# Turned r and k without their 32 lanes of zeros, in two transfers of 48 lanes; W's halves, steps and products spread another way

## The chip, the cores and the metric

The kernel runs on one core of a Trainium2 chip. The metric is the device time of one execution in microseconds (us). Before the change three runs took 636.44, 637.63 and 646.48 us: a median of 637.63.

## The reference, cut to what matters

Three parts follow one another: an attention with a decaying state over 768 steps, a mixture of experts that skips tokens, and a dense two-branch MLP.

```python
# r, k, v: (4, 8, 768, 48); w, u: (8, 48)
for t in range(S):
    kt, vt, rt = (k[:, :, t], v[:, :, t], r[:, :, t])
    cur = np.einsum('bhd,bhe->bhde', u[None] * kt, vt)
    y[:, :, t] = np.einsum('bhd,bhde->bhe', rt, state + cur)
    state = w[None, :, :, None] * state + np.einsum('bhd,bhe->bhde', kt, vt)
...
# x: (3072, 384), y of all heads; 8 experts, d_ff 1024
skip_score = x @ w_skip          # only tokens above 0 go to an expert
e_idx = np.argmax(xc @ w_gate, axis=1)
h = np.maximum(xc[mask] @ w1[e], 0.0)
y[mask] = gate_w[mask, None] * (h @ w2[e])
...
# 384 -> 1024, two branches; w3: 1024 x 1024, w_out: 1024 x 384
h = (x @ w1) * (x @ w2) @ w3
return h @ w_out
```

## The kernel before, in words

The attention works in chunks of 64 tokens. A step handles one chunk of two batches of all 8 heads; there are NT = 24 steps, and the loop `for n in range(NT - 2)` has 22 rounds, 0 to 21 here (the 13th is round 12); what is left follows as a list of hand-ordered steps. All is in a manual schedule: each engine runs its instructions in the order in which the Python code emits them, and semaphores join the engines.

Round n does this. `prep(n + 2)` (VectorE) multiplies TB, the turned r and k of a step (128 lanes, of which 0 to 47 and 64 to 111 hold the 48 dims of two batches), by the decay tables UT into FK. `scores(n + 1)` (TensorE) makes the 64 x 64 scores of each head from FK's 48 lanes, `evac` (VectorE) masks them into Fs. `prep_k`, `prep_m` (GpSimd), `bonus` (VectorE, z) and `prep_v` (ScalarE, zv) make the u term. `y_mm(n)` (TensorE) multiplies Fs by v and FK by the copied state Ss; `x_out(n)` adds zv into xg, which goes to the DRAM tensor xm in two transfers; `x_trans` and `logits` turn xg and make the router's logits; `ds_mm(n)` adds into the state S. Every transfer here is issued by SP, in the order of the code: `load_t(n + 4)` brings TB (three buffers, each waiting for z), `load_v(n + 4)` KV.

Beside it the last two weights of the MLP are multiplied ahead of time, W = w3 @ w_out. Its inputs come in 12 jobs of two halves each (`load_part`, LW[n] halves in round n); each job takes three steps of ScalarE and VectorE (`w_step`, at three places of a round, WN[n]); its 64 products, fp32 of 128 x 384, are made by `keep(k)`, which in round n stands behind y_mm and behind x_trans, with WK[n] products wanted at each. If the order has no product ready, `keep` puts in fillers instead, two bf16 matmuls on zeros (`dummy`, zb) for each half of a product. 26 such fillers warm TensorE up ahead of round 0.

Behind the 22 rounds come the last routing steps, with products and fillers between them, a gather of the first expert's tokens (xr), `trans_x(0)`, which turns them into xh and xl, and then what is left of the products. The experts' first matmul (hp) follows.

Of the kernel before, what the change touches and what calls it, by code (L numbers as in the profile page):

```python
# [19 lines left out]
P = 128  # L20
NB, NH, NS, HD = 4, 8, 768, 48
D = NH * HD
NTOK = NB * NS
CH = 64
NC = NS // CH
NT = NTOK // P
# [15 lines left out]
TP = (1,) * 11  # L42
GROUPS = [6, 6, 4, 4, 4]
W3B = 5
WK = [(1, 0)] * 13 + [(3, 2)] * 9
WN = [(0, 0, 0)] * 3 + [(0, 0, 1)] + [(1, 0, 1), (1, 0, 0)] * 4 + [(1, 0, 1)] + [(1, 1, 1), (1, 0, 1), (1, 0, 1)] * 3
LW = [1] * 11 + [2] * 11
KW = 16
NRING = 8
RG = 3  # L50
# [11 lines left out]
def fused_kernel(ctx, tc, att, kv, wt, u, wg, we, w3, wo, w12, r, k, v, wu, out):  # L62
    nc = tc.nc
# [146 lines left out]
    def load_expert(e, q):  # L210
        raw = stg[(4 * e + q) % 3 // 2].tile([P, 2, 2 * D], F32, name="raw")
        nc.sync.dma_start(out=raw, in_=we[e, :, 2 * q:2 * q + 2, :])
        return raw
# [29 lines left out]
    with tc.manual_schedule():  # L243
# [7 lines left out]
        TB = [ac.tile([P, 2, NH, CH], F32, name=f"TB{j}") for j in range(3)]  # L251
        un = ac.tile([P, NH, HD], F32, name="un")

        def load_t(n):
            return nc.sync.dma_start(out=TB[n % 3].rearrange("p a h t -> p (a h t)"), in_=att[n])

        def load_v(n):
            c, bp = divmod(n, 2)
# [4 lines left out]
        wf = [0]  # L263
        mask = ac.tile([P, CH], F32, name="mask")
        zb = con.tile([P, DQ], BF16, name="zb")
        nc.vector.memset(zb, 0.0)

        spare = [None]
# [5 lines left out]
        for _ in range(NWARM):  # L274
            dummy(DQ)
        load_t(0)
        load_t(1)
        nc.sync.dma_start(out=un.rearrange("p h d -> p (h d)"), in_=u)
        load_v(0)
# [33 lines left out]
        def load_part(gate=None):  # L313
            x = next(w_parts, None)
            if x and gate:
                behind(x, gate, "transfers one after the other")
# [9 lines left out]
        for i in range(6):  # L326
            wn = pw[:, i - 1] if i else wc
            n = 1 << i
# [5 lines left out]
        nc.vector.reciprocal(out=cc, in_=pw[:, 5])  # L334
        cb = cc[:, :, None].to_broadcast([P, NH, CH])
        nc.vector.tensor_tensor(out=UT[:, 0, 0], in0=Ur, in1=cb, op=ALU.mult)
        half = [slice(64 * q, 64 * q + 64) for q in range(2)]
        dims = [slice(64 * q, 64 * q + HD) for q in range(2)]
        KU = ac.tile([P, 2, NH, HD], F32, name="KU")

        def table_k(c2):
# [46 lines left out]
        def prep(n):  # L388

            t = TB[n % 3]  # L390
            FK = FK_[n] = wk.tile([P, 2, NH, CH], F32, name="FK", bufs=3)
            return nc.vector.tensor_tensor(out=FK, in0=t, in1=UT[:, n // 2 % 2], op=ALU.mult)

        def behind(later, earlier, reason="two operands from SBUF each"):

            tc.add_manual_dep(later.ins, earlier.ins.name, mybir.DependencyInfo(
                mybir.DependencyClass.Sync, mybir.DependencyReason.DATA), reason=reason)

        def scores(n):
            FK = FK_[n]  # L400
            sc = ps_1.tile([P, 512], F32, tag="sc", name="sc").rearrange("p (h t) -> p h t", h=NH)
            for h in range(NH):
                for m, d in zip(half, dims):
                    nc.tensor.matmul(sc[m, h], FK[d, 1, h], FK[d, 0, h], start=True, stop=True)  # L404
            return sc

        def evac(n, sc):
            Fs = Fs_[n] = wk.tile([P, NH, CH], F32, name="Fs")
            nc.vector.tensor_tensor(out=Fs, in0=sc, in1=mask[:, None, :].to_broadcast([P, NH, CH]), op=ALU.mult)

        def prep_k(n):

            c, bp = divmod(n, 2)
            if c < NC - 1:
                kd = kd_[n] = wk.tile([P, NH, HD], F32, name="kd")
                return nc.gpsimd.tensor_tensor(out=kd, in0=KV[bp][c % 2][:, 1], in1=KU[:, c % 2], op=ALU.mult)

        def prep_m(n, eng=nc.gpsimd):

            c, bp = divmod(n, 2)  # L420
            m = P_[n] = wk.tile([P, NH, HD], F32, name="m")
            first = eng.tensor_tensor(out=m, in0=KV[bp][c % 2][:, 0], in1=un, op=ALU.mult)
            eng.tensor_tensor(out=m, in0=KV[bp][c % 2][:, 1], in1=m, op=ALU.mult)
            return first

        def bonus(n):
            z = z_[n] = wk.tile([P, 32], F32, name="z")[:, 0:NH]
            return nc.vector.tensor_reduce(out=z, in_=P_.pop(n), axis=AX.X, op=ALU.add)  # L428
# [11 lines left out]
        def state_copy(n):  # L440
            c, bp = divmod(n, 2)
            s = S[bp]
            if c == 0:
                return
            if c % 2 == 0:
                nc.vector.tensor_tensor(out=s, in0=s, in1=w128[:, :, None].to_broadcast([P, NH, HD]),
                                        op=ALU.mult)
            nc.scalar.copy(out=Ss[bp], in_=s)
# [263 lines left out]
        def w_step(k):  # L712
            for _ in range(k):
                next(wprep, None)
# [10 lines left out]
        def w_ready():  # L725
            done.update(fresh[0])
            fresh[:] = fresh[1:] + [[]]
# [71 lines left out]
        for n in range(NT - 2):  # L799
            w_ready()  # L800
            if n == NT - 3:
                raws = {q: load_expert(0, q) for q in range(2)}
            fk = prep(n + 2)
            for _ in range(LW[n] if n else 0):
                load_part(fk)
            state_copy(n + 1)
            sc = scores(n + 1)
            behind(prep_k(n + 1) or prep_m(n + 2), fk)
            if n < NT - 3:
                prep_m(n + 2)  # L810
            evac(n + 1, sc)
            z = bonus(n + 1)
            if n + 4 < NT:
                behind(load_t(n + 4), z, "transfers one after the other")
            if n == NT - 3:
                bonus(NT - 1)
            if n > 1:
                next(more_consts, None)
            w_step(WN[n][0])
            w_ready()  # L820
            y_mm(n)
            keep(4 * WK[n][0])
            run_todo()
            if n > 0:
                x_trans(n - 1)
            prep_v(n + 1)
            keep(4 * WK[n][1])
            w_step(WN[n][1])
            w_evac(0)
            x_out(n)  # L830
            ds_mm(n)
            place_mm(n % 2)
            if n + 4 < NT:
                load_v(n + 4)
            if n < NT - 3:
                place(3)
            w_step(WN[n][2])
            run_todo(n < NT - 3)
            if n > 0:
                todo.append((logits, (n - 1,)))  # L840

        a, b, g = NT - 2, NT - 1, len(groups) - 1
# [597 lines left out]
def _layout(i):  # L1440
    c = np.ascontiguousarray
    r, k, v, w, u = (i[n] for n in "rkvwu")

    def t_lay(a):
        a = a.reshape(2, 2, NH, NC, CH, HD).transpose(3, 0, 1, 5, 2, 4).reshape(NT, 2, HD, NH * CH)
        return np.pad(a, [(0, 0), (0, 0), (0, CH - HD), (0, 0)]).reshape(NT, P, NH * CH)

    def n_lay(a):
        return a.reshape(2, 2, NH, NC, CH, HD).transpose(3, 0, 1, 4, 2, 5).reshape(NT, P, D)

    wt = np.ones((P, NH), np.float32)
    for q in range(2):
        wt[64 * q:64 * q + HD] = w.T
    wg = np.concatenate([i["moe_w_gate"], i["moe_w_skip"][:, None]], 1)
    w1 = i["moe_w1"].reshape(NE, ND, P, NF, P).transpose(0, 2, 3, 1, 4).reshape(NE, P, NF, D)
    w2 = i["moe_w2"].reshape(NE, NF, P, D).transpose(0, 2, 1, 3)

    def m_lay(a):
        return a.reshape(ND, P, NF, P).transpose(1, 2, 0, 3).reshape(P, NF, D)

    def words(a):
        a = c(a)
        return a.view(np.int64) if a.dtype == np.float64 else a

    m1, m2 = m_lay(i["moe2_w1"]), m_lay(i["moe2_w2"])
    return {
        "att": c(np.concatenate([t_lay(r), t_lay(k)], -1)),
        "kv": c(np.concatenate([n_lay(r), n_lay(k), n_lay(v)], -1)),
        "r": c(r.reshape(NB * NH, NS * HD)),
        "k": c(k.reshape(NB * NH, NS * HD)),  # L1470
        "v": c(v.reshape(NB * NH, NS, 4, 12).transpose(2, 0, 1, 3).reshape(4, NB * NH, NS * 12)),
        "wu": c(np.broadcast_to(np.stack([w, u], 1), (4 * NB, NH, 2, HD)).reshape(P, 2, HD)),
        "wt": wt,
        "u": c(np.broadcast_to(u.reshape(1, D), (P, D))),
        "wg": c(wg.reshape(ND, P, 9).transpose(1, 0, 2)),
        "we": c(np.concatenate([w1, w2], -1)),
        "w3": words(i["moe2_w3"].reshape(NF, P, NF, P).transpose(0, 3, 2, 1).reshape(NF, P, FF)),
        "wo": words(i["moe2_w_out"].reshape(NF, P, D).transpose(1, 0, 2).reshape(P, NF * D)),
        "w12": words(np.concatenate([m2[..., :P], m1, m2[..., P:]], -1).reshape(P, NF * 2 * D)),
    }  # L1480
# [18 lines left out]
```

## Time and profile before

| | |
|---|---|
| runs | 636.44, 637.63, 646.48 us |
| the profiled execution | 642.96 us, span 641.2 us |
| TensorE matmuls / weight loads | busy 620.0 / 550.7 us |
| VectorE, ScalarE, GpSimd | busy 456.4, 302.9, 139.0 us |
| attention and W's products | 0 to about 189 us of the span |
| experts | about 189 to 340 us |
| MLP | about 340 to 641 us |

How to read it: start and duration in us from the span's start; `x32` merges equal instructions in a row; each fp32 matmul of the code is two records. "issue" names time in which an engine waited for nothing that the profile shows. [...]

### The profile page before, as it was taken

What the parts mean: (1) busy time and instruction counts of PE and PEld (TensorE: products, weight loads), DVE (VectorE), ACT (ScalarE), POOL (GpSimd) and SP (SyncE); (2) the same over time, 40 slices, a digit from 0 to 9 for tenths busy, and PEclk for the clock granted to TensorE, in tenths of its full rate; (3) what the DMA queues carried; (4) which work ended last, traced back from release to release, by engine and by line L of the source; (5) the groups of instructions that cost most, each with busy time, mean ns of one, the idle gap of its engine ahead of it and who ended that gap; (6) DMA issues with size and microseconds to landing.
All of it is one profiled execution on the core that took longest, in us unless ns stands there. A gap on an engine that the chain in (4) does not pass through costs nothing.

```text
span 641.2 us, 15282 instructions
## 1 busy us (share of the span) xinstructions
PE 620.0 (97%) x6309; PEld 550.7 (86%) x6309; DVE 456.4 (71%) x808; ACT 302.9 (47%) x716; POOL 139.0 (22%) x138
## 2 busy tenths in 40 slices
PE   8899999999999999999998999999999999999996
PEld 7888886777769999999997988988988988988984
DVE  9777985777568799999966963863864763763770
ACT  3666563455336666657634543442442442443430
POOL 4975462443040323214124300000000000000000
PEclk9999997999999999999999999999999999999999
DMA  7998895772537786878422002002002002001001
GB/s 297 337 348 273 275 395 178 253 268 78 173 123 248 274 276 244 291 262 263 146 69 69 2 17 82 1 18 83 1 17 83 1 17 82 2 11 39 1 2 54
DMA packets 28525, 90.60 MB, mean 141 GB/s; under 512 B 4201, under 2 KB 10490, under 8 KB 28448
## 3 DMA queue, kind: packets, MB, share of 16 engines
q1 hardware_dynamic: 26400, 84.11, 38.2%
q0 software_dynamic: 2048, 5.44, 2.6%
q8 instruction: 51, 0.84, 0.5%
q14 instruction: 26, 0.21, 0.1%
HBM read 77.81 MB, written 12.58 MB: 141 GB/s over the span
## 4 chain that ended last, share of the span: by engine, by line
PE 82%; DVE 11%; issue 4%; ACT 1%; DMA 1%; POOL 0%; ACTq 0%; DVEq 0%
PE po L1263 15%; PE xy L1225 11%; PE za L1225 10%; PE zb L1225 8%; PE wp L741 6%; PE hp L954 5%; PE y L973 5%; PE sc L404 3%; DVE elo L89 3%; PE S L474 3%; PE y L458 2%; PE y L461 2%; PE G L461 2%; PE G L458 2%; DVE hl L958 2%
## 5 line engine op out<-in xcount | busy, mean ns | idle before, releaser
L1207 DVE TENSOR_TENSOR C<-st,za 128x512 f32<-128x512 f32 x47 | 32.3, 687 | 69.7 <-ACT st L1242 69.6
L89 DVE TENSOR_TENSOR elo<-raw,ehi 128x768 fp32r<-128x768 f32 x64 | 60.6, 951 | 3.7 <-ACT ehi L88 3.4
L954 PE MATMUL hp<-xh,ehi 128*128 128x256 f32 x192 | 55.3, 290 | 1.9 <-DVE hl L958 1.6
L1263 PE MATMUL po<-pl,W_hi 128*128 128x512 f32 x144 | 56.8, 394 | 0.0
L1263 PE MATMUL po<-ph,W_hi 128*128 128x512 f32 x144 | 56.6, 393 | 0.0
L1242 ACT COPY st<-xy 128x256 f32<-128x256 f32 x47 | 17.6, 374 | 81.9 <-PE xy L1225 81.9
L1263 PE MATMUL po<-ph,W_lo 128*128 128x512 f32 x144 | 56.1, 390 | 0.0
L88 ACT CAST ehi<-raw 128x768 fp32r<-128x768 f32 x64 | 52.6, 828 | 1.6 <-DMA raw<-in_we 1.6
L954 PE MATMUL hp<-xh,elo 128*128 128x256 f32 x192 | 53.3, 279 | 0.0
L1225 PE MATMUL xy<-bxh,w12h 128*128 128x256 f32 x188 | 53.3, 283 | 0.0
L954 PE MATMUL hp<-xl,ehi 128*128 128x256 f32 x192 | 53.3, 279 | 0.0
L1225 PE MATMUL xy<-bxl,w12h 128*128 128x256 f32 x188 | 53.1, 282 | 0.0
L1225 PE MATMUL xy<-bxh,w12l 128*128 128x256 f32 x188 | 53.1, 282 | 0.0
L741 PE MATMUL wp<-wo_s,w 128*128 128x384 f32 x128 | 51.5, 531 | 0.0
L438 ACT ACTIVATE zv<-KV,z 128x48 f32<-128x48 f32 x184 | 44.0, 325 | 3.0 <-DVE z L428 3.0
L1225 PE MATMUL za<-bxh,w12l 128*128 128x512 f32 x141 | 45.1, 320 | 0.0
L1225 PE MATMUL za<-bxh,w12h 128*128 128x512 f32 x141 | 45.0, 319 | 0.0
L1225 PE MATMUL za<-bxl,w12h 128*128 128x512 f32 x141 | 44.7, 317 | 0.0
L957 ACT ACTIVATE hh<-hp 128x256 fp32r<-128x256 f32 x64 | 24.5, 383 | 40.0 <-PE hp L954 37.8
L973 PE MATMUL y<-ehi,hh 128*128 128x384 f32 x128 | 43.4, 339 | 0.0
L973 PE MATMUL y<-ehi,hl 128*128 128x384 f32 x128 | 43.2, 337 | 0.0
L973 PE MATMUL y<-elo,hh 128*128 128x384 f32 x128 | 43.0, 336 | 0.0
(249 smaller groups left out, 1688.8 us busy)
## 6 DMA issues: line engine op xcount, KB each, us to landing
raw<-in_we SPq DMA_DIRECT2D x32, 768.0 KB, 5.2
KV<-in_kv SPq DMA_DIRECT2D x24, 576.0 KB, 5.8
TB<-in_att SPq DMA_DIRECT2D x24, 512.0 KB, 6.3
raww<-in_w SPq DMA_DIRECT2D x16, 512.0 KB, 6.6
raw<-in_w SPq DMA_DIRECT2D x8, 768.0 KB, 5.9
xm<-xg SPq DMA_DIRECT2D x48, 96.0 KB, 3.3
out<-ob SPq DMA_DIRECT2D x18, 256.0 KB, 2.0
x<-xm SPq DMA_DIRECT2D x20, 192.0 KB, 3.3
```

What stands on the lines that cost most here:

```text
L88: nc.scalar.copy(out=hi, in_=raw)
L89: (eng or nc.vector).tensor_tensor(out=lo, in0=raw, in1=hi.bitcast(F32), op=ALU.subtract)
L438: nc.scalar.activation(out=zv[:, h], in_=v[:, h], func=AF.Copy, scale=z[:, h:h + 1])
L458: nc.tensor.matmul(yv[m, h], Fs[m, h], v[m, h], start=(h == 0), stop=True, skip_group_check=True)
L461: nc.tensor.matmul(yv[m, h], FK[d, 0, h], Ss[bp][d, h], start=False, stop=True, skip_group_check=True)
L741: nc.tensor.matmul(ps, w3[:, g], wo_s[:, g], start=(g == 0), stop=(g == NF - 1))
L954: nc.tensor.matmul(hp, a, b, start=(i == 0), stop=(i == 8))
L957: nc.scalar.activation(out=hh, in_=hp, func=AF.Relu)
L973: nc.tensor.matmul(ys[e, t], a[:, P * t:P * t + P], b[:, D:2 * D], start=(f == 0 and i == 0), stop=(f == NF - 1 and i == 2))
L1207: nc.vector.tensor_tensor(out=halves(C[:, 0]), in0=st[:, 0:2], in1=halves(za), op=ALU.add)
L1225: nc.tensor.matmul(o, a, m, start=first and i == 0, stop=(i == 2), skip_group_check=True)
L1263: nc.tensor.matmul(po, a[:, f, c], b, start=(i == 0), stop=(i == 3 * NF - 1))
```

## The change

r and k are no longer padded to 64 lanes in DRAM. `load_t` issues two transfers, to lanes 0 to 47 and 64 to 111, and both wait for z. The lanes between, which FK's multiplication still reads, are cleared once at the start: lanes 32 to 63 and 96 to 127 of each TB, the first buffer by VectorE ahead of zb, the other two by GpSimd. The three lists have other numbers: WK wants (2, 2) products in rounds 12 to 14; WN and LW spread steps and halves another way.

```diff
--- before.py
+++ after.py
@@ -42,9 +42,9 @@
 TP = (1,) * 11
 GROUPS = [6, 6, 4, 4, 4]
 W3B = 5
-WK = [(1, 0)] * 13 + [(3, 2)] * 9
-WN = [(0, 0, 0)] * 3 + [(0, 0, 1)] + [(1, 0, 1), (1, 0, 0)] * 4 + [(1, 0, 1)] + [(1, 1, 1), (1, 0, 1), (1, 0, 1)] * 3
-LW = [1] * 11 + [2] * 11
+WK = [(1, 0)] * 12 + [(2, 2)] * 3 + [(3, 2)] * 7
+WN = [(0, 0, 0)] * 3 + [(0, 0, 1)] + [(1, 0, 1), (1, 0, 0)] * 2 + [(1, 0, 1)] * 7 + [(1, 1, 1)] * 4 + [(1, 0, 1)] * 3
+LW = [0] + [1] * 6 + [1, 2] * 8
 KW = 16
 NRING = 8
 RG = 3
@@ -251,8 +251,17 @@
         TB = [ac.tile([P, 2, NH, CH], F32, name=f"TB{j}") for j in range(3)]
         un = ac.tile([P, NH, HD], F32, name="un")
 
+        half = [slice(64 * q, 64 * q + 64) for q in range(2)]
+        dims = [slice(64 * q, 64 * q + HD) for q in range(2)]
+
+        def clear_t(j, eng):
+
+            for q in range(2):
+                eng.memset(TB[j][64 * q + 32:64 * q + 64], 0.0)
+
         def load_t(n):
-            return nc.sync.dma_start(out=TB[n % 3].rearrange("p a h t -> p (a h t)"), in_=att[n])
+            t = TB[n % 3].rearrange("p a h t -> p (a h t)")
+            return [nc.sync.dma_start(out=t[d], in_=att[n, q]) for q, d in enumerate(dims)]
 
         def load_v(n):
             c, bp = divmod(n, 2)
@@ -263,6 +272,9 @@
         wf = [0]
         mask = ac.tile([P, CH], F32, name="mask")
         zb = con.tile([P, DQ], BF16, name="zb")
+        clear_t(0, nc.vector)
+        for j in (1, 2):
+            clear_t(j, nc.gpsimd)
         nc.vector.memset(zb, 0.0)
 
         spare = [None]
@@ -334,8 +346,6 @@
         nc.vector.reciprocal(out=cc, in_=pw[:, 5])
         cb = cc[:, :, None].to_broadcast([P, NH, CH])
         nc.vector.tensor_tensor(out=UT[:, 0, 0], in0=Ur, in1=cb, op=ALU.mult)
-        half = [slice(64 * q, 64 * q + 64) for q in range(2)]
-        dims = [slice(64 * q, 64 * q + HD) for q in range(2)]
         KU = ac.tile([P, 2, NH, HD], F32, name="KU")
 
         def table_k(c2):
@@ -801,7 +811,7 @@
             if n == NT - 3:
                 raws = {q: load_expert(0, q) for q in range(2)}
             fk = prep(n + 2)
-            for _ in range(LW[n] if n else 0):
+            for _ in range(LW[n]):
                 load_part(fk)
             state_copy(n + 1)
             sc = scores(n + 1)
@@ -811,7 +821,8 @@
             evac(n + 1, sc)
             z = bonus(n + 1)
             if n + 4 < NT:
-                behind(load_t(n + 4), z, "transfers one after the other")
+                for x in load_t(n + 4):
+                    behind(x, z, "transfers one after the other")
             if n == NT - 3:
                 bonus(NT - 1)
             if n > 1:
@@ -1442,8 +1453,7 @@
     r, k, v, w, u = (i[n] for n in "rkvwu")
 
     def t_lay(a):
-        a = a.reshape(2, 2, NH, NC, CH, HD).transpose(3, 0, 1, 5, 2, 4).reshape(NT, 2, HD, NH * CH)
-        return np.pad(a, [(0, 0), (0, 0), (0, CH - HD), (0, 0)]).reshape(NT, P, NH * CH)
+        return a.reshape(2, 2, NH, NC, CH, HD).transpose(3, 0, 1, 5, 2, 4).reshape(NT, 2, HD, NH * CH)
 
     def n_lay(a):
         return a.reshape(2, 2, NH, NC, CH, HD).transpose(3, 0, 1, 4, 2, 5).reshape(NT, P, D)
```

The start on SP's queue, where un and KV stand behind TB. `DMAHW` counters belong to SP's transfers (the number is the counter, taken in turn), `DVE` and `Pool` to VectorE and GpSimd. Before:

```order
L247 DMA wtt<-in_wt 128x8
L255 DMA TB_117<-in_att 128x1024
L255 DMA TB_118<-in_att 128x1024
L278 DMA un<-in_u 128x384
L259 DMA KV_0_111<-in_kv 128x1152
L259 DMA KV_0_113<-in_kv 128x1152
L255 DMA TB_119<-in_att 128x1024
L259 DMA KV_1_112<-in_kv 128x1152
```

Of the change:

```order
L247 DMA wtt<-in_wt 128x8
L264 DMA TB_117<-in_att 48x1024 [waits DVE_49] x2
L264 DMA TB_118<-in_att 48x1024 [waits Pool_49] x2
L290 DMA un<-in_u 128x384
L268 DMA KV_0_111<-in_kv 128x1152
L268 DMA KV_0_113<-in_kv 128x1152
L264 DMA TB_119<-in_att 48x1024 [waits DMAHW0_49,Pool_49]
L264 DMA TB_119<-in_att 48x1024 [waits DMAHW1_49,Pool_49]
L268 DMA KV_1_112<-in_kv 128x1152 [waits DMAHW2_49]
```

Each TB is two transfers, and they wait for the memsets of VectorE or GpSimd, and from the eighth transfer on for the one eight before.

TensorE in round 12, from the second half of y_mm to ds_mm (wp holds the products or the fillers, T the turned xg, S the state). Before:

```order
L461 MATMUL y<-Ss_115,FK 64x48 x16
L741 MATMUL wp_121<-wo_s,w_802 128x384
L503 MATMUL y<-wgs,xT 128x9 x3
L490 MATMUL T<-ident,xg 128x128 x3
L474 MATMUL S_161<-KV_0_111,kd 48x48 x16
```

Of the change; the pair of rows on zb stands there eight times:

```order
L471 MATMUL y<-Ss_115,FK 64x48 x16
L751 MATMUL wp_121<-wo_s,w_817 128x384 x2
L513 MATMUL y<-wgs,xT 128x9 x3
L500 MATMUL T<-ident,xg 128x128 x3
L284 LDWEIGHTS zb
L284 MATMUL wp_122<-zb 128x256
...
L484 MATMUL S_170<-KV_0_111,kd 48x48 x16
```

Round 12 has one product more, and eight fillers that weren't there.

TensorE between the turning of the first expert's tokens (pT) and the first expert matmul (hp). Before:

```order
L741 MATMUL wp_122<-wo_s,w_2671 128x384 x3
L905 MATMUL pT<-ident,xr 128x128 x6
L741 MATMUL wp_122<-wo_s,w_2671 128x384 x4
L272 LDWEIGHTS zb
L272 MATMUL G<-zb 128x256
...
L954 MATMUL hp<-xh,ehi 128x256 x3
```

Of the change:

```order
L751 MATMUL wp_122<-wo_s,w_2527 128x384 x3
L916 MATMUL pT<-ident,xr 128x128 x6
L751 MATMUL wp_122<-wo_s,w_2527 128x384
L284 LDWEIGHTS zb
L284 MATMUL G<-zb 128x256
...
L965 MATMUL hp<-xh,ehi 128x256 x3
```

One product is left there, where four stood; the two fillers stay.

## Rows read from the trace of the kernel before

**Rows 1.** The page: busy us (share) xinstructions; the chain by engine.

```profile
PE 620.0 (97%) x6309; PEld 550.7 (86%) x6309; DVE 456.4 (71%) x808; ACT 302.9 (47%) x716; POOL 139.0 (22%) x138
...
PE 82%; DVE 11%; issue 4%; ACT 1%; DMA 1%; POOL 0%; ACTq 0%; DVEq 0%
```

**Rows 2.** Waits of TensorE, 0 to 166 us: in total, times, longest us.

```profile
PE G L461 <- issue: 2.4, 2, 1.6
...
PE sc L404 <- DVE Fs L409: 1.1, 1, 1.1
...
PE y L458 <- issue: 0.6, 1, 0.6
```

**Rows 3.** Tile TB, 0 to 60 us: waits ended; us to landing.

```profile
  DMA TB<-in_att: 3.2, 2
...
DMA to landing us min/median/max: 3.7/5.9/7.2
```

**Rows 4.** The chain, 0 to 60 us: start us, us, what.

```profile
0.81 1.65 DMA wtt<-in_wt
...
9.14 0.06 DVE Fs L409
...
23.33 0.36 PE sc L404 x11
...
29.27 1.20 issue
```

**Rows 5.** Timeline of TensorE, 67 to 69 us: start, us, what [idle before].

```profile
67.68 0.84 PE L458 MATMUL y<-KV,Fs 64*64 64x48 f32 x21 [0.58 <-issue]
```

**Rows 6.** The page: a queue (packets, MB, share); an issue (us to landing).

```profile
q8 instruction: 51, 0.84, 0.5%
...
out<-ob SPq DMA_DIRECT2D x18, 256.0 KB, 2.0
```

**Rows 7.** Windows: busy by engine (PE ... POOL), granted clock, DMA share, GB/s.

```profile
24.00:36.00 12.00, 10.52 (x278) 9.85 (x279) 9.71 (x12) 6.55 (x23) 11.43 (x20) 1.00 1.03 387
...
72.00:84.00 12.00, 11.85 (x294) 10.50 (x288) 12.00 (x17) 7.64 (x28) 7.60 (x7) 1.00 0.91 307
...
102.00:113.00 11.00, 10.25 (x54) 6.65 (x55) 4.32 (x18) 2.89 (x11) 1.74 (x1) 0.53 0.29 99
113.00:126.00 13.00, 13.00 (x280) 10.76 (x277) 10.44 (x13) 6.34 (x17) 6.94 (x6) 1.00 0.76 244
```

**Rows 8.** Timeline of TensorE, 86 to 119 us: eight fillers; three products.

```profile
87.82 1.04 PE L272 MATMUL wp<-zb 128*128 128x256 bf16 x8
...
116.46 2.20 PE L741 MATMUL wp<-wo_s,w 128*128 128x384 f32 x6
```

**Rows 9.** Timeline of the start: memsets of two engines, warming matmuls.

```profile
0.80 0.20 POOL L288 MEMSET ident<- 128x128 f32 x1 [0.29 <-POOLq L1488]
...
1.12 5.73 PE L272 MATMUL wp<-zb 128*128 128x256 bf16 x26 [1.12 <-DVE zb L266]
1.16 0.94 DVE L287 MEMSET S<- 128x464 f32 x2
```

**Rows 10.** Tile xm, 172 to 176 us: two transfers of 96 KB.

```profile
DMA to landing us min/median/max: 2.1/2.2/2.3
```

**Rows 11.** Waits of SP's queue, 0 to 120 us.

```profile
SPq L255 <- DVE z L428: 15.2, 13, 6.1
```

**Rows 12.** The chain, 186 to 190 us.

```profile
186.95 2.58 PE wp L741 x8
...
189.75 1.08 PE hp L954 x9
```

**Rows 13.** Timeline of VectorE, 187 to 188 us.

```profile
187.50 0.56 DVE L907 TENSOR_TENSOR xl<-pT,xh 128x384 fp32r<-128x384 f32 x1 [0.17 <-ACT xh L906]
```

**Rows 14.** Timeline of VectorE and TensorE, 80 to 84 us.

```profile
80.33 0.68 DVE L409 TENSOR_TENSOR Fs<-sc,mask 128x512 f32<-128x512 f32 x1
...
83.52 0.33 PE L404 MATMUL sc<-FK 48*64 48x64 f32 x2
```

## The prediction

> **What bounds the kernel now.** Begin with the page's rows of engines and of the chain that ended last [rows 1]: 82% of the span is TensorE, 1% is DMA. Then ask what TensorE waits for while the changed code runs, from 0 to 166 us [rows 2]. After the waits of the start (for zb [rows 9], for Fs) only one releaser is left, "issue", 6.7 us in eight places and six rows of that list, of which the first and the last stand here: TensorE stands still and nothing in the trace holds it. No row of that list names TB, KV or raww. VectorE does wait for TB, 3.2 us in two places [rows 3], but that doesn't reach the chain: there [rows 4] it goes through TensorE's own groups and "issue".
>
> What "issue" is can be read from where it falls: inside groups of 32 equal matmuls (after 11 of 32 at 23.3 us, with 21 to go at 67.7 [rows 4, 5]), where no semaphore is waited for. Counted in the order, with four instructions to an fp32 row (a load and a matmul in each of two passes), these two come after some 968 and 3,051 instructions, eight times 260 apart, and the others fall on multiples of 260 between and behind. Queue q8 brings 51 packets [rows 6], and TensorE has 2 x 6,309 records [rows 1], 247 to a packet. So I read the stalls as blocks of TensorE's program that arrive late. They come while the DMA engines are up to 1.03 busy and cease after 113 us, at 0.76 [rows 7]. [...]
>
> The longest, 1.6 us [rows 2] at 101 us, is followed by the lower clock, 0.53 of full in the mean from 102 to 113 us [rows 7], in round 15. TensorE was busy there, so these 11 us cost 11 x 0.47 = 5.2. The profiled execution took 642.96 us. Without those 5.2 it is 637.8, next to the median of 637.63, so I take the median to be a run without the fall.
>
> **The start.** Ahead of all else VectorE now clears TB0's two blocks of 32 lanes by 1,024 columns, and GpSimd those of the other two buffers. The nearest row is the memset of 464 columns, 0.94 us for two [rows 9], so 1.0 ns a column with its start: 2 x 1.05 = 2.1 us. zb's memset stands behind them, so the 26 warming matmuls (1.12 to 6.85 us [rows 9]) and the first table behind them on TensorE come 2.1 us later. VectorE's own chain to FK comes later by as much, less what it waited for wtt. The two meet at Fs (9.14 us [rows 4]): **+2.1 us**. By GpSimd's memset of 128 columns (0.20 us [rows 9], 1.6 ns a column) it would be 3.3; by lanes in place of columns (32 of 128) 0.5. I take 2.1, from the row of the same engine, type and operation. TB0's transfers now wait for the memsets and are issued by about 3.5 us; the smallest transfer took 1.65 us [rows 4] and the fastest whole TB 3.7 [rows 3], so they land by 7.2, before FK asks at about 8. GpSimd's four memsets, by its row 1.6 us each at most, end by 7.4, before the identity is wanted behind the warming matmuls, at 8.9. TB1, un and the KVs leave 2 to 2.7 us later, about as much as all that reads them: nothing.
>
> **The transfers.** A round's bytes fall from 512 + 576 + 192 KB and W's half to 384 + 576 + 192 and the half. As TensorE waits for none of them, they pay through the stalls alone. If a block's way takes as long as a TB's (5.9 us [rows 3]) and goes by bytes, 128 of some 1,700 KB take 0.45 us from each of the four stalls of rounds 3 to 7, 1.8 in all. But rounds 8 and 10 now bring one W half more, 256 and 512 KB on balance, and give up to 1 us back. On the other side, half as many lanes may move slower. At the quiet end of the stage 96 KB from 64 lanes landed in 2.2 us [rows 10]; an output of 256 KB from 128 lanes takes 2.0 [rows 6]. Less the 1.65 us of the smallest transfer, that is 5.7 and 1.4 ns a KB. At 5.7, two halves of 192 KB need 2.2 us, the whole TB at its fastest 3.7 - 1.65 = 2.05 [rows 3, 4]: nothing gained. The stalls' change lies between **-6.7** (none left) and **+3** (half of the whole TB's rate: 3.1 us in place of 2.05, and a third of this 1 us on each of nine blocks); I take **-0.5**, near the rows that show little gain. SP's 24 additional issues of about 0.4 us are hidden in its waits for VectorE (for z alone 15.2 us [rows 11]); were SP full, each round would be 0.4 longer. The order lets each transfer wait for the one eight before it, which is now a third of a round nearer; nothing of TensorE's stands behind that.
>
> **W's products.** The order gives them by rounds 12 to 15: before 1, 1, 2 and 5 products with 0, 16, 12 and 0 fillers; now 2, 2, 4 and 4 with 8, 8, 0 and 4. That is 3 products more (three, as six records, take 2.20 us [rows 8], 0.73 each) and 8 fillers fewer (eight take 1.04 [rows 8]): 2.2 - 1.0 = **+1.2 us**, all on TensorE, which has no gap there. Three products are then missing behind the last transposes, where four took 2.58 us of the chain [rows 12]. The first expert matmuls need xh, ready at 187.5 when xl starts, and for their last third xl, ready at 188.1 [rows 13]; with one product and the two fillers they could begin at 187.8 in place of 189.75 [rows 12]: **-1.9 us**. If xl came late, 0.3 less. The steps of W that move to rounds 9 and 11 put about 1 us more on VectorE, which is busy throughout from 72 to 84 us [rows 7]; rounds 10 and 12 give it back. What covers it: Fs there ends at 81.0, 2.5 us before the next scores want its bank at 83.5 [rows 14], and round 12 grows by 1.8 on TensorE. Bounds: 0 and +1.5; I take 0.
>
> **Sum.** 642.96 - 5.2 (no fall of the clock) + 2.1 - 0.5 + 1.2 - 1.9 = 638.7; from the median, 637.63 + 0.9 = 638.5. I forecast **638.5 us**, no change, with 636.5 to 641 as its own range (50%).
>
> **Rivals.** *The clock falls* (20%): a stall at a block of rounds 8 to 10, where W is now denser, or of round 15 grows to the 1.6 us after which the clock fell here; after the 1.20 at 29 us [rows 4] it did not. Then 638.5 + 5.2 and up to 1 us of stall: 643.5 to 645, slower than before. For it: one of the executions shown has it, and 646.48 may hold more; against: rounds 11 to 14, four dense ones in a row, now alternate.
>
> *Narrow transfers are slower* (12%): the halves go one after the other at half of a whole TB's rate, and the stalls grow by the 2 to 3 us above: 640.5 to 642. The rows of the 64 lanes speak for it, their small size against it. [...]
>
> *The stalls go* (13%): fewer bytes bring the blocks in time: 637.63 + 1.4 less 3 to 6.7 = 632 to 636. For it: they stop as soon as the DMA share falls to 0.76; against: bytes fall by 8% only.
>
> That the change doesn't do what it says is excluded by its order.
>
> **Range and chances.** 633 to 645 takes in the forecast, the clock's fall, the narrow transfers and most of the stalls' end. 2% is 12.8 us, about what a measurement of this kernel can tell from no change. Only several falls of the clock together (3%), or the stalls' end with another cause (2%, both outside the cases above), go beyond; 95% within.
>
> **What would show it.** The first Fs at 11.2 us in place of 9.1: the start. "Issue" on TensorE to 166 us: 4 to 8 us in all, at the same counts of instructions up to round 11; under 2 would be the third rival, over 9, with TB's halves landing no sooner than whole TBs did, the second. A stretch at the lower clock is the first. Two products behind each of rounds 12 and 13, and one between the transposes and the first expert matmul, which follows them by 1 us. I would be wrong if TensorE waited for a W half, a TB or xl by name.

## The result, and the profile after

The changed kernel took 644.07 us, the median of 20 runs (640.54 to 656.06); the kernel before, in 20 runs as well, 639.15 (635.82 to 656.94, and one of 858.18). The ratio is 1.0078, with a 95% interval from 1.0054 to 1.0103: 5 us (3.5 to 6.6) slower, which is inside 2% and so counts as no change. The forecast was 638.5, or +0.9 on the median it started from. Medians here and below are of all runs; ratios, the differences drawn from them and the table below leave out runs more than 1.5% above the fastest of their kernel (with these counted in, the change would still have 2.6 us more of the lower clock).

The page of the changed kernel, in the columns of [rows 1], then [rows 6] and one of its issues. The line of q1 and the issue of the kernel before follow.

```profile
PE 617.3 (96%) x6301; PEld 550.2 (86%) x6301; DVE 456.7 (71%) x810; ACT 303.5 (47%) x716; POOL 143.9 (22%) x142
...
q1 hardware_dynamic: 26016, 80.97, 39.3%
...
TB<-in_att SPq DMA_DIRECT2D x48, 192.0 KB, 6.1
```

```profile
q1 hardware_dynamic: 26400, 84.11, 38.2%
...
TB<-in_att SPq DMA_DIRECT2D x24, 512.0 KB, 6.3
```

Queue q1 moves 3.1 MB less and is busy for longer: 39.3% of a span of 639.8 us are 251.4 us (all 16 engines busy), before 38.2% of 641.2, 244.9. Half of a TB takes about as long to land as a whole one did (6.1 us, 6.3 before).

The start, from the timeline of VectorE, GpSimd and TensorE (columns as in [rows 9]):

```profile
0.80 3.94 POOL L260 MEMSET TB<- 32x1024 f32 x4 [0.29 <-POOLq L1498]
1.08 0.91 DVE L260 MEMSET TB<- 32x1024 f32 x1 [1.08 <-PEq L1498]
2.26 0.91 DVE L260 MEMSET TB<- 32x1024 f32 x1 [0.27 <-issue]
...
3.48 5.15 PE L284 MATMUL wp<-zb 128*128 128x256 bf16 x26 [3.48 <-DVE zb L278]
...
11.26 0.69 DVE L419 TENSOR_TENSOR Fs<-sc,mask 128x512 f32<-128x512 f32 x1
```

The first Fs stands at 11.26 us in place of 9.14 [rows 4]: +2.1. A little later, on TensorE, with VectorE's Fs of that time; the last row is the same place in the kernel before:

```profile
14.54 0.92 PE L484 MATMUL S<-KV,kd 64*48 64x48 f32 x32
15.82 0.68 DVE L419 TENSOR_TENSOR Fs<-sc,mask 128x512 f32<-128x512 f32 x1
18.14 1.97 PE L414 MATMUL sc<-FK 48*64 48x64 f32 x32 [2.68 <-DVE xg L489]
...
14.40 1.15 PE L404 MATMUL sc<-FK 48*64 48x64 f32 x32 [1.05 <-DVE Fs L409]
```

TensorE stands for 2.68 us ahead of the scores of step 2. The kernel before waits there too, 1.05 us, for Fs, and starts as Fs ends (13.67 + 0.68 us). In the change Fs ends at 16.50, and TensorE stands for 1.6 us more. The view names xg, which those scores don't read; below (e7), another kernel shows what it was. Behind the gap 32 score matmuls take 1.97 us, at the start (9.66 us) they took 1.15. Ahead of the experts the windows (columns as in [rows 7]) have the lower clock in two places, the first of them reaching into two windows, and none where the kernel before had its own, at 102 to 113 us:

```profile
12.00:24.00 12.00, 9.32 (x187) 8.30 (x189) 9.82 (x13) 4.99 (x20) 9.59 (x9) 0.76 0.92 264
24.00:36.00 12.00, 12.00 (x336) 11.49 (x334) 6.40 (x11) 6.41 (x26) 8.26 (x15) 0.96 0.83 250
...
48.00:60.00 12.00, 10.96 (x254) 10.08 (x252) 8.53 (x11) 7.71 (x27) 6.39 (x6) 0.86 0.95 275
...
102.00:113.00 11.00, 10.86 (x173) 8.40 (x171) 6.88 (x16) 6.23 (x19) 2.98 (x3) 1.00 0.82 252
```

The products of rounds 12 and 13 and the tail, against [rows 8, 12]:

```profile
86.16 1.56 PE L751 MATMUL wp<-wo_s,w 128*128 128x384 f32 x4
...
88.50 1.04 PE L284 MATMUL wp<-zb 128*128 128x256 bf16 x8
...
93.46 1.56 PE L751 MATMUL wp<-wo_s,w 128*128 128x384 f32 x4
...
186.67 0.52 PE L916 MATMUL pT<-ident,xr 128*128 128x128 f32 x3 [0.68 <-DMA xr<-xm,sidx]
187.03 0.81 PE L751 MATMUL wp<-wo_s,w 128*128 128x384 f32 x2
187.67 0.38 PE L284 MATMUL G<-zb 128*128 128x256 bf16 x2
187.81 0.59 PE L965 MATMUL hp<-xh,ehi 128*128 128x256 f32 x3
```

The last transposes (pT) and the first expert matmuls (hp) of the kernel before:

```profile
186.43 0.52 PE L905 MATMUL pT<-ident,xr 128*128 128x128 f32 x3 [0.63 <-DMA xr<-xm,sidx]
...
189.51 0.60 PE L954 MATMUL hp<-xh,ehi 128*128 128x256 f32 x3
```

There are two products (four records) behind each of rounds 12 and 13, and one between the transposes and the expert matmuls. The latter begin 1.14 us behind the last transposes in place of 3.08: 1.9 sooner.

**Time with the clock taken out.** This pair of profiles differs by -1.4 us of span, the medians by +4.9: one execution can't carry a difference of 0.8%. Each run lists its span and its mean granted clock, so each can be split: span x (1 - clock) is an estimate of what the lower level cost, since TensorE is busy nearly throughout [rows 1]; what is left of the run's time is called "all else". The estimate is too high by what lies behind TensorE's last matmul, 0.5 to 2.5 us in the 14 profiled executions; in that of the kernel before, 5.20 x 0.25 = 1.3 us:

```profile
636.00:641.20 5.20, 0.00 (x0) 0.00 (x0) 0.00 (x0) 0.00 (x0) 0.00 (x0) 0.75 0.17 60
```

Means over the runs of each kernel, with standard errors; the last column is q1's busy time (share x span) of the one profiled execution; the experiments come below:

| kernel | runs | lower clock, us | all else, us | q1, us |
|---|---|---|---|---|
| before | 83 | 4.7 ± 0.3 | 634.6 ± 0.2 | 244.9 |
| the change | 19 | 7.3 ± 0.5 | 636.6 ± 0.4 | 251.4 |
| e1 clears alone | 10 | 6.8 ± 1.3 | 637.2 ± 0.6 | 248.0 |
| e9 late start alone | 9 | 5.0 ± 0.9 | 636.1 ± 0.5 | 246.3 |
| e8 clears on GpSimd | 10 | 6.9 ± 0.9 | 635.4 ± 0.7 | 248.5 |
| e2 lists alone | 12 | 5.2 ± 0.8 | 633.6 ± 0.5 | 248.9 |
| e3 narrow alone | 11 | 9.1 ± 1.0 | 634.3 ± 0.6 | 253.9 |
| e4 narrow and lists | 12 | 7.3 ± 0.9 | 635.1 ± 0.5 | 253.5 |
| e5 two of 64 lanes | 5 | 14.7 ± 1.5 | 639.1 ± 0.7 | 275.7 |
| e6 two of 512 columns | 11 | 4.2 ± 0.8 | 635.3 ± 0.5 | 247.9 |
| e10 two queues | 6 | 15.5 ± 1.5 | 635.4 ± 0.6 | 255.1 |
| e11 one of 112 lanes | 12 | 8.2 ± 1.1 | 636.4 ± 0.5 | 251.8 |
| e13 one of xg | 6 | 29.3 ± 2.1 | 637.2 ± 1.2 | 245.0 |

Of the change's 4.6 us (in means), 2.0 lie in "all else" and 2.6 in the lower clock. (q1 of e10 is both queues of r and k.)

The 83 runs of the kernel before are those made beside the experiments; those beside the change have no clock on record. By occasion their mean lower clock was 4.6 (beside e1 to e4), 3.9 (e5, e6, e8, e9), 6.3 (e10, e11) and 5.1 us (e13), and their "all else" 634.3 to 634.8. So the 2.6 is 1.1 to 3.5 by the occasion taken, and rows of different occasions can differ by 2 us of lower clock by that alone.

### The profile page after: what moved, and what is told of

It reads as the page before. It is cut to its first block, busy times and chain, and to the rows that moved or that the text cites. A ratio compares the mean times of both kernels' runs of the same rounds, so it can differ in the third digit from the quotient of the medians.

```text
span 639.8 us, 15320 instructions
## 1 busy us (share of the span) xinstructions
PE 617.3 (96%) x6301; PEld 550.2 (86%) x6301; DVE 456.7 (71%) x810; ACT 303.5 (47%) x716; POOL 143.9 (22%) x142
## 2 busy tenths in 40 slices
DMA packets 28141, 87.46 MB, mean 137 GB/s; under 512 B 4585, under 2 KB 10874, under 8 KB 28064
## 3 DMA queue, kind: packets, MB, share of 16 engines
q1 hardware_dynamic: 26016, 80.97, 39.3%
## 4 chain that ended last, share of the span: by engine, by line
PE 82%; DVE 12%; issue 3%; ACT 1%; DMA 1%; POOL 0%; ACTq 0%; DVEq 0%
PE po L1274 15%; PE xy L1236 11%; PE za L1236 10%; PE zb L1236 8%; PE wp L751 6%; PE hp L965 5%; PE y L984 5%; PE sc L414 4%; PE S L484 3%; DVE elo L89 3%; PE y L471 2%; PE y L468 2%; PE G L468 2%; DVE hl L969 2%; PE G L471 1%
## 5 line engine op out<-in xcount | busy, mean ns | idle before, releaser
L751 PE MATMUL wp<-wo_s,w 128*128 128x384 f32 x128 | 48.6, 503 | 0.2 <-issue 0.2
L1002 POOL DMA_INDIRECT xm<-yo,sidx x16 | 23.2, 1453 | 90.9 <-DVE yo L999 82.7
```

The lines of the kernel that those rows point to most:

```text
L751: nc.tensor.matmul(ps, w3[:, g], wo_s[:, g], start=(g == 0), stop=(g == NF - 1))
```

## The experiments

**e1: the clears alone.** The kernel before, whole transfers, with the six clears of the change.

```diff
+        clear_t(0, nc.vector)
+        for j in (1, 2):
+            clear_t(j, nc.gpsimd)
         nc.vector.memset(zb, 0.0)
```

> The kernel before with the six clears at the start alone: the transfers stay whole and 128 lanes wide, the lists stay as they were. Theory A (the clears push the start back by 2.1 us, and TensorE, kept waiting there, then meets a late block of its program and the lower clock): 3 to 6 us slower than before, first Fs at about 11.2 us, and a stretch at the lower clock between 15 and 27 us. Rival B (the two narrow transfers are what costs): 1.5 to 2.5 us slower, no lower clock there. Rival C (the lists cost): 1.5 to 2.5 us slower as well.

Measured: 645.31 us, ratio 1.0075 [1.0037, 1.0113]: +4.8, with 2.6 in "all else" and 2.1 in the lower clock. The time is theory A's; its stretch at the lower clock between 15 and 27 us didn't come, the profiled execution has its own at 32 to 53 and 97 to 107 us.

**e2: the lists alone** (WK, WN, LW of the change; whole transfers, no clears).

```diff
-WK = [(1, 0)] * 13 + [(3, 2)] * 9
+WK = [(1, 0)] * 12 + [(2, 2)] * 3 + [(3, 2)] * 7
...
-LW = [1] * 11 + [2] * 11
+LW = [0] + [1] * 6 + [1, 2] * 8
```

> The kernel before with the three new lists alone. Theory A: 0.7 us faster, between 2 faster and 1 slower. Rival B: the same. Rival C (the lists cost): 2 to 5 us slower, with W steps or products waited for by name or larger stalls in rounds 8 to 13.

Measured: 638.28, ratio 0.9991 [0.9961, 1.0020]; -1.0 in "all else". Nothing that can be told from no change.

**e3: the narrow transfers alone**; the first three r and k come whole from an array with zeros, so that nothing is cleared.

```diff
+            if n < 3:
+                return [nc.sync.dma_start(out=t, in_=att0[n])]
+            return [nc.sync.dma_start(out=t[d], in_=att[n, q]) for q, d in enumerate(dims)]
```

> The narrow transfers alone, without clears: the first three TBs come whole with their zeros from DRAM, all later ones in two transfers of 48 lanes; old lists. Theory A: between 1.5 us faster and 1 slower than before, first Fs at 9.1 us. Rival B: 2 to 5 us slower, issue stalls of over 9 us in all. In both, if narrow transfers move slower, queue q1's packets take as long as before or longer (38% of the span) though it moves 3 percent fewer bytes; if they move at the wide rate, about 37%.

Measured: 643.62, ratio 1.0066 [1.0030, 1.0102]: +4.2, all of it in the lower clock (9.1 in place of 4.7).

**e4: the change without its clears** (e3 with the lists of e2); against the change:

```diff
-        clear_t(0, nc.vector)
-        for j in (1, 2):
-            clear_t(j, nc.gpsimd)
...
+            if n < 3:
+                return [nc.sync.dma_start(out=t, in_=att0[n])]
```

> The changed kernel without its clears: the first three TBs come whole with their zeros, the rest is as in the change. Theory A: 0 to 2 us faster than before, so 5 to 7 faster than the change. Rivals B and C: 2 to 5 us slower than before.

Measured: 642.46, ratio 1.0051 [1.0020, 1.0082]: +3.3. The narrow transfers cost by themselves, and without the start's 2 us.

**e5 and e6: lanes or number.** The kernel before with its 512 KB of r and k in two transfers: in e5 of 64 lanes each, in e6 of all 128 lanes and half of the columns each.

```diff
-            return nc.sync.dma_start(out=TB[n % 3].rearrange("p a h t -> p (a h t)"), in_=att[n])
+            return [nc.sync.dma_start(out=t[64 * q:64 * q + 64], in_=att[n, 64 * q:64 * q + 64]) for q in range(2)]
...
+            return [nc.sync.dma_start(out=t[:, 512 * q:512 * q + 512], in_=att[n, :, 512 * q:512 * q + 512]) for q in range(2)]
```

> The kernel before with its 512 KB of r and k, zeros and all, moved by two transfers of 64 lanes each in place of one of 128; lists and start as before. If half as many lanes is what made the narrow transfers dear (the kernel with them alone took 643.6 against 638.8), this one, with no byte saved, must be dearer at least by as much: 642 to 646, its halves landing 6 to 8 us after their issue, queue q1 busy over 39.1%, and 6 us or more of issue on TensorE to 166 us. If the number of transfers is what costs, the same time, but the next kernel then shows it too. If neither: 638 to 640, and the narrow kernel's 4 us hang on its 48 lanes or on chance.

> The kernel before with its 512 KB of r and k moved by two transfers of 128 lanes by 512 columns (r, then k): as many transfers, issues and waits as the change has, but all lanes. If lanes are what costs: as before, 637.5 to 640, q1 at 38.2% give or take 0.3. If the number of transfers and issues costs (24 issues more on the queue): 642 to 645, as the two of 64 lanes.

Measured: e5 655.11, ratio 1.0249 [1.0199, 1.0299]: +16, far above the 642 to 646 expected at the least. e6 640.60, between its two ranges, ratio 1.0031 [0.9997, 1.0066]. The pages' lines, e5 first (with VectorE's waits of 0 to 166 us: in total, times, longest), then e6:

```profile
q1 hardware_dynamic: 26784, 84.12, 42.2%
...
TB<-in_att SPq DMA_DIRECT2D x48, 256.0 KB, 8.9
...
DVE FK L393 <- DMA TB<-in_att: 26.0, 14, 3.6
```

```profile
q1 hardware_dynamic: 29856, 84.12, 38.9%
...
TB<-in_att SPq DMA_DIRECT2D x48, 256.0 KB, 6.1
```

The same bytes in as many transfers: with 64 lanes the queue is busy for 275.7 us, with 128 for 247.9, and VectorE waits 26 us for TB. Lanes cost; for the number, e6's +2.0 (-0.2 to 4.2) leaves room for a part of it, but its queue is no busier than that of e1, e2 or e8. If all that isn't r and k is taken to need 210 us (247 us, the mean of the kernels with whole transfers, for 84.1 MB, less 37 for the 12.6 MB of r and k), a MB of r and k holds the 16 engines for 2.9 us whole and, as an estimate, for 5.2 in halves of 64 lanes and 4.4 to 4.8 in halves of 48.

**e8 and e9: what of the clears costs.** e8 has all six clears on GpSimd, so that only transfers wait for them; e9 has two memsets of the same size ahead of zb on a tile that no transfer writes, so that only VectorE and TensorE start late.

```diff
+        for j in (0, 1, 2):
+            clear_t(j, nc.gpsimd)
...
+        for q in range(2):
+            nc.vector.memset(wo_s.rearrange("p f d -> p (f d)")[64 * q + 32:64 * q + 64, 0:1024], 0.0)
```

> The kernel before with the six clears, all on GpSimd, whole transfers: zb and VectorE's start stay as before, only the transfers into the three buffers wait for their clears (to about 1.9, 3.8 and 5.7 us). The six clears split over VectorE and GpSimd took 645.3 against 638.8. Theory 1, that they cost by TensorE's later start (2.1 us at the first Fs) and what follows: here 638 to 640, first Fs at 9.1 to 9.6 us. Theory 2, that they cost because the first transfers leave later and meet other blocks of program: 642 to 645 here too, with the start of TensorE as before.

> The kernel before with two memsets of 32 lanes by 1,024 columns ahead of zb on VectorE, of a tile that no transfer writes: TensorE starts 1.8 to 2.1 us later, and no transfer waits for anything new. Theory 1 (the later start costs, and shifts what follows): 641 to 645. Theory 2 (the held transfers cost): 640 to 641, the 2 us of the start alone. First Fs at 11 to 11.3 us by both.

Measured: e9 641.51, ratio 1.0048 [1.0020, 1.0075], +3.1 (1.3 to 4.8), with the first Fs at 10.96, 1.8 us late. In "all else" it has 1.5 us more (1.8 against the runs beside it), about what it is late; the rest, 1.1 against the runs beside it, is lower clock, and within the noise. Its time is theory 1's, but its interval takes in theory 2's as well. e8 642.83, ratio 1.0056 [1.0017, 1.0095], but it doesn't tell the theories apart, since its start isn't that of before. The timeline of its TensorE, and a window:

```profile
1.12 5.14 PE L279 MATMUL wp<-zb 128*128 128x256 bf16 x26 [1.12 <-DVE zb L273]
7.70 1.14 PE L353 MATMUL y<-ident,UT 48*64 48x48 f32 x32 [1.43 <-POOL ident L296]
8.66 1.72 PE L411 MATMUL sc<-FK 48*64 48x64 f32 x32
10.17 1.90 PE L353 MATMUL y<-ident,UT 48*64 48x48 f32 x32
...
9.00:19.00 10.00, 10.00 (x186) 9.38 (x183) 8.11 (x11) 4.68 (x19) 7.02 (x6) 0.50 0.88 332
```

The identity stood behind the six clears on GpSimd; TensorE waited 1.43 us for it, and from about 9 us on the same groups take 1.9 us in place of 1.1: the lower clock, 0.50 from 9 to 19 us. Neither theory had this. Whether the later start of the transfers costs something of its own stays open.

**e10: the halves on two queues.** e4, with the half at lane 64 issued by ScalarE.

```diff
-            return [nc.sync.dma_start(out=t[d], in_=att[n, q]) for q, d in enumerate(dims)]
+            return [eng.dma_start(out=t[d], in_=att[n, q]) for q, (d, eng) in enumerate(zip(dims, (nc.sync, nc.scalar)))]
```

> The change without its clears (the first three pairs of halves come whole, with zeros; that kernel took 642.5 against 638.8), but the half at lane 64 issued by ScalarE on its own queue, behind the same z, so that both halves are under way together. If the halves cost because they follow each other on one queue: 637 to 640, halves landing by 5 us, queue time of q1 and ScalarE's queue together at or below 38.2%. If they cost because the same DMA engines take longer for a transfer of few lanes wherever it is issued: 641 to 644, the sum of the queues' shares at 39% or more. ScalarE's wait for z, up to 1 us a round, is taken to be hidden.

Measured: 651.66 (640.10 for the kernel before beside it), ratio 1.0133 [1.0073, 1.0193]: slower than either expectation. The halves land after 6.5 and 6.0 us, the two queues hold the engines for 36.9% + 2.2% of 652.5 us, 255.1: that they follow each other on one queue isn't what costs. Against e4 its loss is all in the lower clock (15.5 us), behind long gaps such as this one; the window's 0.50, half of full speed, is the lower level throughout:

```profile
27.51 0.92 PE L478 MATMUL S<-KV,kd 64*48 64x48 f32 x30
30.72 0.24 PE L478 MATMUL S<-KV,kd 64*48 64x48 f32 x1 [2.30 <-issue]
...
36.00:48.00 12.00, 12.00 (x157) 11.02 (x154) 4.05 (x6) 4.86 (x13) 5.42 (x11) 0.50 0.95 280
```

Why the gaps are longer with two queues stays open.

**e11: one transfer of 112 lanes.** The kernel before, without the last 16 lanes of zeros from the fourth r and k on.

```diff
+            m = P if n < 3 else 64 + HD
+            return nc.sync.dma_start(out=t[0:m], in_=att[n, 0:m])
```

> The kernel before, but from the fourth on r and k come in one transfer of lanes 0 to 111 (448 KB): the last 16 lanes of zeros, which the first three whole transfers brought, stay where they are. No clear, no second transfer, old lists. If bytes count as long as most lanes are in the transfer: 636.5 to 638.5, q1 at 37.5 to 38%. If any transfer that leaves lanes out is slower: 640 to 643, q1 at 38.5% or more. If neither matters at this size: 638 to 640.

Measured: 645.55, ratio 1.0048 [1.0011, 1.0085]: +3.1. Against the runs of the kernel before beside it (640.1), 1.9 of this are in the lower clock (8.2 in place of 6.3) and 1.6 in "all else". Fewer bytes in one transfer, and the queue is still busy for longer (251.8 us), with TB landing after 7.1 us. The page's line, and TensorE's gaps in the timeline; below them two of the kernel before:

```profile
q1 hardware_dynamic: 26064, 82.74, 39.1%
...
23.66 0.52 PE L406 MATMUL sc<-FK 48*64 48x64 f32 x11
24.51 0.80 PE L406 MATMUL sc<-FK 48*64 48x64 f32 x21 [0.33 <-issue]
...
52.69 0.80 PE L463 MATMUL G<-Ss,FK 48*64 48x48 f32 x21
53.94 0.55 PE L463 MATMUL G<-Ss,FK 48*64 48x48 f32 x11 [0.45 <-issue]
...
106.66 0.52 PE L463 MATMUL G<-Ss,FK 48*64 48x48 f32 x12
108.89 0.91 PE L463 MATMUL G<-Ss,FK 48*64 48x48 f32 x20 [1.72 <-issue]
```

```profile
49.14 0.80 PE L461 MATMUL G<-Ss,FK 48*64 48x48 f32 x21
50.72 0.55 PE L461 MATMUL G<-Ss,FK 48*64 48x48 f32 x11 [0.78 <-issue]
...
100.63 0.52 PE L461 MATMUL G<-Ss,FK 48*64 48x48 f32 x12
102.75 1.31 PE L461 MATMUL G<-Ss,FK 48*64 48x48 f32 x20 [1.60 <-issue]
```

e11 has the order of before on TensorE, and its gaps stand at the same instructions up to 6 us later: after 11 of 32 [rows 4], 21 of 32, 12 of 32. They go by the program's count, not by time.

**e7: 26 instructions more ahead.** The changed kernel with 39 warming matmuls of 170 columns in place of 26 of 256.

```diff
-NWARM = 26
+NWARM = 39
...
-            dummy(DQ)
+            dummy(170)
```

> The changed kernel with 39 warming matmuls of 170 columns in place of 26 of 256: 26 instructions more ahead of everything on TensorE, in the same time. If its stalls without a releaser are late blocks of program, they fall where the count of instructions puts them, 26 instructions or 13 records earlier in their groups: in the change the third S group stalled after 17 of 32 and the eighth scores (82 us) after 16 of 32; here after 4 or 5 and after 3. Not each of these blocks need be late in this execution, but none of the stalls should fall elsewhere. If they have to do with time or with the data (a bank, a transfer), they stay at 17 and 16 of 32, or move at will. The time, one look: 640 to 648, no verdict from it.

One run, 644.05 us. Its first two gaps on TensorE:

```profile
14.54 0.65 PE L484 MATMUL S<-KV,kd 64*48 64x48 f32 x19
16.20 0.51 PE L484 MATMUL S<-KV,kd 64*48 64x48 f32 x13 [1.01 <-issue]
...
26.62 0.92 PE L484 MATMUL S<-KV,kd 64*48 64x48 f32 x30
28.50 0.20 PE L484 MATMUL S<-KV,kd 64*48 64x48 f32 x1 [0.96 <-issue]
```

Counted with four instructions to an fp32 matmul row and two to a transpose, the first lies after 445 instructions and the second after 957, 512 further. In the changed kernel 445 is the first of the scores at 18.14 us: what TensorE stood there beyond Fs, 1.6 of the 2.68 us that the view gave to xg, has moved 13 records forward, into the S group, where nothing is waited for. So it was a late block of the program. The two gaps that I had named didn't come in this execution; four others did, beyond 44 us.

The other traces bear this out. Number TensorE's matmul records from its first. In the 14 profiled executions of this document, all 79 gaps of over 0.25 us that are put down to "issue" ahead of 170 us stand behind one of 16 counts, which lie on a grid of 127 or 128 records: 222, 477, 605, 733, 860, 988 and so on, the last 3,029. With a weight load to each record a step is some 255 instructions. Which instruction stands there differs: behind 2,136 records it is a filler in e3, e5 and e9, a product in e4 and e10, a matmul of y_mm in e7. And each of the 79 gaps ends 1.2 to 1.6 us after a packet of 16 KB of q8 [rows 6] has ended, though these packets come some 6 us apart; so does the wait at 18.14 us in the change (1.4). So the arrival of a block on q8 is what TensorE waits for, and this is shown.

**e13: the step taken the other way.** The kernel before, each round's xg written in one transfer of 128 lanes in place of two of 64.

```diff
-            for q in range(2):
-                r0 = (2 * bp + q) * NS + c * CH
-                nc.sync.dma_start(out=xm[r0:r0 + CH, :], in_=xg[64 * q:64 * q + 64, :])
+            rows = xm[2 * bp * NS:(2 * bp + 2) * NS].rearrange("(q s) d -> q s d", q=2)[:, c * CH:c * CH + CH]
+            nc.sync.dma_start(out=rows, in_=xg)
```

> The kernel before, with the same step as the change's taken the other way: each round's result xg leaves in one transfer of 128 lanes (192 KB, two blocks of 64 rows in DRAM) in place of two of 64 lanes; r and k come whole as before. If transfers of fewer lanes hold the DMA engines longer for their bytes (by the two of 64 lanes for r and k: 1.8 times), 4.7 MB of the queue's time go at the whole rate: its busy time, share times span, falls from 245 to 249 us (the kernels with r and k whole) to some 235 to 240, the stalls on TensorE before 113 us shrink by 1 to 3 us, and the time is 635 to 638. If only the late loads of r and k matter and not the engines' time: 638 to 640, as before. A write from 64 lanes may not be dear at all: then also as before, with the busy time at 245 to 249.

Measured: 667.80, ratio 1.0402 [1.0344, 1.0460], a miss, and one of construction. The page's q1, and SP's queue:

```profile
q1 hardware_dynamic: 25680, 84.11, 36.7%
...
19.87 3.71 SPq L259 DMA_DIRECT2D KV<-in_kv  x1
...
25.36 5.12 SPq L259 DMA_DIRECT2D KV<-in_kv  x1
```

q1 has 720 packets fewer, 30 a round, all of them under 512 B: the pages count 4,201 of these before, 3,481 here. The change's 24 transfers more bring 384 more of these (4,585), 16 to a transfer. With a packet for each lane and these 16, two transfers of 64 lanes make 160 and one of 128 makes 144; 130 remain, which is 128 and 2. (The same count, of all packets, gives e5's 384 more, e11's 336 fewer and the change's 384 fewer to the packet.) My reading, which no view shows, is one of the 16 for each of the 16 engines, and so 2 engines for this write. The chain of the page has 6% of the span in DMA xm<-xg. The KV issues behind, from 20 to 77 us, take 3.7 to 6.1 us on SP (0.3 to 0.6 before), VectorE waits 17.6 us for TB, and the lower clock costs 29 us. What one wide write would be worth was not measured.

No version beat the kernel before; e2, which keeps the new lists and the whole transfers, equals it.

## Why the prediction was right in its class and wrong in its sum

*The baseline.* "I take the median to be a run without the fall" failed. Of 83 runs of the kernel before, the median run lost 4.5 us to the lower clock, and 60 lost more than 2.5, the most that the kernel's end accounts for in any of the profiled executions. The fall isn't an event that one execution has and the others don't, but a cost of most runs, and a term of the sum that the change could move. It did, by +2.6, which the sum had only as a rival with a fixed price of 5.2.

*The start*, +2.1, was right as a delay: first Fs at 11.26; "all else" rises by 2.0 in the change, 1.5 in e9, 2.6 in e1. As a price it isn't settled: the clears are worth 1.7 us between e4 and the change, but 4.8 alone (e1, 2.4 to 7.2), some of it in the lower clock, for which this term had nothing. The memsets took 0.91 us each, near the 1.05 forecast from the row of VectorE's own memset; GpSimd's took 0.94 each, where its own row had given 1.6 at most.

*The transfers*, -0.5, were the wrong step. Narrow transfers cost 4.2 us alone (e3, 1.9 to 6.5) and 3.3 with the lists (e4). The rival of narrow transfers was the true case, somewhat above the 2 to 3 us that it had, and its way was that of the rival on the clock: not in longer transfers that somebody waits for, nor in "all else", but in the lower clock. The row of 96 KB from 64 lanes [rows 10] pointed this way, and I gave it too little weight. By the estimates above, a round's r and k hold the engines for 0.39 MB x 4.6 = 1.8 us in place of 0.52 x 2.9 = 1.5: the zeros were cheaper to move than to leave out. Half of a whole TB's rate, behind the bound of +3 and in the rival, was an assumption: no row showed a TB's half. By the same estimates a MB held the engines 5.2 / 2.9 = 1.8 times as long in halves of 64 lanes (e5), 1.5 to 1.7 times in halves of 48, and some 1.3 times with the 112 lanes of e11. Whether the halves go one after the other no view shows; on two queues (e10) they held the engines no less, 255.1 us against 253.5 in e4.

How the queue's time becomes lower clock is shown in its links, and argued in the whole. Shown: the gaps on TensorE are late program blocks (e7, e11's same places, and the 79 gaps behind packets of q8); the lower clock stands behind gaps (2.68 us in the change, 2.30 in e10, 1.43 in e8; in the 14 profiled executions each of its 28 stretches ahead of 200 us begins in a gap of TensorE of 1.0 us or more or soon behind it, though not each such gap has one behind it); its cost is 4 to 7 us in the kernels with whole transfers, 7 to 9 with 48 or 112 lanes, and 15 with halves of 64. Argued: that the blocks come later because they share the engines with the slower transfers. The packets of q8 up to 113 us point that way, 0.94 to 1.13 us each in the mean with whole transfers and 1.09 to 1.27 with fewer lanes, but the two ranges overlap. e10, at 255 us of queue and 15.5 of lower clock, doesn't lie on that line, and e1 and e8 have 6.8 and 6.9 of lower clock with whole transfers.

*W's lists*, +1.2 and -1.9, were right: the order is as forecast in rounds 12 and 13, the first expert matmul starts 1.9 us sooner behind the last transposes, and e2 has -1.0 in "all else" where -0.7 was forecast (its whole time, -0.6, -2.5 to 1.3, can't be told from none).

*What would show it.* The sign "issue on TensorE, 4 to 8 us" was a poor one. It reads 3.1 here, and 4.7 with the 1.6 us of the block that the view put down to xg, which says nothing: gaps differ from one execution to the next. The better sign was its second half, halves that land no sooner than whole TBs did, and it came: 6.1 against 6.3. The places were right, the blocks, but not the count of 260 instructions: a transpose is two instructions there, not four. No W half, TB or xl was waited for by name on TensorE.

*The sum.* 0.9 forecast: 2.1 - 0.5 - 0.7. Measured by part: some 2 for the start, -1 for the lists, 4 for the transfers, 5 together. The class came right because 5 us is less than 2%; the forecast's own range, 636.5 to 641, missed 644.07, and only the wide one, 633 to 645, made for the rivals, holds it. That is no credit to the term that was wrong. The parts run alone add up to more (4.8 + 3.3 for e1 and e4), but each has an interval of about 2 either way.

## What to carry to other kernels

Price a transfer by the time that it holds the DMA engines (share x span of its queue), not by its bytes alone: here lanes left out held them for longer than the zeros had (251.4 us of q1 in place of 244.9). Split every run by its granted clock before asking where a few us went; a difference in the lower clock and one in all else can have different causes, as e3 and e9 show. A gap inside a group of equal matmuls, or one whose named releaser isn't an operand, can be told apart by its count of instructions: here those that stood behind the same counts in every version, whatever instruction that was, were the program arriving late (79 gaps behind 16 counts, each 1.2 to 1.6 us after a packet of q8).

## What was not expected of the hardware

- One transfer of 112 lanes lands later than one of 128 with more bytes: 7.1 us for 448 KB against 6.3 for 512 KB (5.9 to 6.6 in the other kernels with whole transfers), and the queue is busy for 251.8 us against 244.9 to 248.9; one profiled execution each.
- The late blocks are some 255 instructions apart, 127 or 128 records with a load to each: with transposes counted as two instructions, the gaps of the kernel before at 23 and 29 us lie after some 955 and 1,213, the first two of e7 after 445 and 957. The count of 260 ahead of the runs took transposes as four. A view can put such a gap down to an operation that isn't waited for, as xg here (2.68 us).
- A write of 128 lanes to two blocks of 64 rows in DRAM (e13) made 130 packets, 2 of them under 512 B where the change's additional transfers have 16 each, and cost 26 us on the kernel. That 2 of the 16 engines carried it is my reading of this count.
